# Lead-in of a fused linear-attention and gated-MLP kernel: 64x64 state products, one scaling on GpSimd, two copies on VectorE, constants for the idle products

## Chip, cores and metric

One core of one Trainium2 chip. The time is the device time of one launch in microseconds; the kernel before has a median of 202.86 us over three runs (202.58 to 203.15). Every other time below comes from one profiled execution of it.

## The reference

```python
def _attn_ref(q, k, v, lam):              # q, k, v: [4, 8, 768, 64]; block = 64
    ...
    for b in range(nb):
        intra = einsum('bhic,bhjc->bhij', qb, kb) * Dmask      # lam**(i-j) for i >= j, else 0
        intra = einsum('bhij,bhjd->bhid', intra, vb)
        inter = einsum('bhid,bhde->bhie', qb * lam_pow, kv_state)
        out[:, :, sl] = intra + inter
        kv_state = lam_block * kv_state + einsum('bhsd,bhse->bhde', kb * rev_pow, vb)

def _moe_ref(x, w_in, w_out):             # x: [3072, 512], w_in: [512, 2048], w_out: [2048, 512]
    h = x @ w_in
    return (h * cos(h)) @ w_out
```

x is the attention output with the heads side by side, one row for each token.

## The kernel before

The powers of lam are folded into scales: q is multiplied by lam**pos, k or v by lam**-pos, with pos counted from the middle of the sequence, so that the decay mask becomes a plain causal one and the running state a plain sum of k.T v. Tokens go in blocks of 128. The gated MLP works on tiles of four or two blocks (`TILES`): for each of 16 groups of 128 hidden columns, f0 to f15, L732 multiplies x (held transposed, `xT`) by `w_in`, ScalarE takes the cosine (L738), VectorE multiplies (L744), and L778 multiplies by `w_out`.

The order of instructions isn't that of the program text. Every piece of work is a `Task` with an engine, an assumed duration, dependencies and a priority; `Planner.order` (L72) simulates the engines with these numbers, with assumed delays between engines (`LAT`) and with the times from which each engine is free (`SETUP`), and the tasks are emitted in the order of their planned starts. So a changed duration or engine in the plan can also change the order on each engine.

**The lead-in.** The first four blocks, which make the first MLP tile, don't take the ordinary way but the one of `add_span` (L579): a span is the first 256 tokens of a batch, two tokens to a partition, and there are two spans, x0 and x1. SyncE issues the loads of q and k of x0, then of x1 (L253; 512 KB each). GpSimd's queue issues v of both, then the first two chunks of `w_in` (two groups of columns each, f0 and f1, f2 and f3), then GpSimd scales k of x1, and only then issues the other four chunks (one, three, four and four groups: f4; f5 to f7; and so on) and `w_out`. All tasks of a span split the heads in two halves, hp0 and hp1:

- `prep` (L592) scales q and k into bf16. The table `QK` (L32) names the engine by span and half.
- `transposes` (L596) turns q and k on TensorE, four 128x128 products for each half; `transposes_out` (L603) copies them out of PSUM, by `OUTS` all on ScalarE.
- `scores` (L606), 16 products 64x64 of 128 columns for each half; `scores_out` (L616) applies the mask, two VectorE instructions for each half.
- `update` (L620) forms the state of the span's first block, `ps_kv`: for each pair of heads and each s a product with 64 rows and 128 columns of the array, of which only the two diagonal 64x64 blocks are used. `update_out` (L628) copies these blocks into `kv_bd`, whose other parts were set to zero; `STATE_OUT` (L34) names the engines.
- `values` (L631), 16 products for each half; `carried` (L642), four products with `kv_bd` on top; `values_out` (L648) copies the two blocks of the span to `xT`; `VALUES_OUT` (L33) names the engines.

While TensorE would wait in the lead-in, `keep_awake` (L861) has it multiply constants into a bank that nobody reads. It uses a float32 tile of zeros, `blank`, that VectorE sets first (L215), or for pauses from 0.25 to 0.6 us the identity. Before the first transposes stands the product that spreads lam over the partitions (L875), from which ScalarE computes the scales.

Of the kernel before, what the change touches and what calls it, by code (L numbers as in the profile page):

```python
# [10 lines left out]
F32 = mybir.dt.float32  # L11
BF16 = mybir.dt.bfloat16
# [16 lines left out]
APART = [3, 4, 5, 11]  # L29


QK = [{"q": ("DVE", "DVE"), "k": ("DVE", "DVE")}, {"q": ("DVE", "DVE"), "k": ("POOL", "POOL")}]  # L32
OUTS = [{"qT": ("ACT", "ACT"), "kT": ("ACT", "ACT")}, {"qT": ("ACT", "ACT"), "kT": ("ACT", "ACT")}]  # L33
VALUES_OUT = [("ACT", "ACT"), ("DVE", "ACT")]  # L34
STATE_OUT = [("ACT", "ACT"), ("ACT", "ACT")]
ORDER = "q0 k0 q1 k1 v0 v1 i0 i1 i2 i3 i4 i5 o0 o1 o2 q4 q5 k4 k5 o3"

W_IN = [2, 2, 1, 3, 4, 4]
# [18 lines left out]
class Planner:  # L57


    LAT = {"PE": 0.2, "ACT": 0.06, "DVE": 0.08, "POOL": 0.1, "SP": 0.0, "DMA": 0.0, "SETUP": 0.0}  # L60

    SETUP = {"POOL": 3.7, "DVE": 4.4, "ACT": 6.0, "SP": 0.85, "DMA": 1.95}

    def __init__(self, bufs):
        self.tasks, self.bufs = [], bufs
# [6 lines left out]
    def order(self):  # L72
        free, done = dict(self.SETUP), []
        got = {tag: [] for tag in self.bufs}
        owner = [None] * BANKS
        only = {}
        todo = list(self.tasks)
        while todo:
            first = {}
            for t in todo:  # L80
                if only.get(t.eng, t) is not t:
                    continue
                at = self.ready(t, got)
                if at is None:
                    continue
                if t.banks:
                    b = self.free_banks(t, owner)
                    if len(b) < t.banks:
                        continue
                    t.bank = b[:t.banks]  # L90
                    at = max([at] + [x for x, _ in t.bank])
                at = max(at, free.get(t.eng, 0.0))
                first.setdefault(t.eng, []).append((at, t))
            best = None
            for eng, c in first.items():
                t0 = min(a for a, _ in c)
                a, t = min(((a, t) for a, t in c if a <= t0 + 1e-6 + t.worth), key=lambda x: x[1].issue.end if eng == "DMA" else x[1].prio)
                if best is None or a < best[0]:
                    best = (a, t)
            assert best, "no task can start"  # L100
            a, t = best
            t.start, t.end = a, a + t.dur
            free[t.eng] = t.end
            only.pop(t.eng, None)
            if t.then:
                only[t.eng] = t.then
            if t.get:
                got[t.get].append(t)
            if t.banks:
                t.bank = [i for _, i in t.bank]  # L110
                for j, i in enumerate(t.bank):
                    owner[i] = (t, j)
            todo.remove(t)
            done.append(t)
        return sorted(done, key=lambda t: t.start)
# [29 lines left out]
def kernel(  # L145
# [10 lines left out]
    nc = tc.nc  # L156
    B, H, S, D = q.shape
    P = 128
# [19 lines left out]
    consts = ctx.enter_context(tc.tile_pool(name="consts", bufs=1))  # L178
# [5 lines left out]
    def bank(i, shape, dt, name):  # L184
        return psum.tile(shape, dt, tag=f"bank{i}", bufs=1, name=name)
# [9 lines left out]
    ident = consts.tile([P, P], BF16)  # L195
# [15 lines left out]
                                base=0, pattern=[[1, D]], channel_multiplier=-1)  # L211
    halfpi = consts.tile([P, 1], F32)
    nc.vector.memset(halfpi, math.pi / 2.0)
    blank = consts.tile([P, 4 * P], F32)
    nc.vector.memset(blank, 0.0)  # L215
    kv_bd = consts.tile([P, 2, NP, P], BF16)
    nc.vector.memset(kv_bd, 0.0)

# [8 lines left out]
    pl = Planner({**BUFS, "q_f": BUFS["ld"], "k_f": BUFS["ld"], "v_f": BUFS["ld"]})  # L227
# [3 lines left out]
    halves = [slice(i * D, (i + 1) * D) for i in range(2)]  # L231
# [344 lines left out]
    spans, span_deps = [], []  # L576
    span_v = [consts.tile([P, H, 2, D], BF16, name=f"v_sp{x}") for x in range(SPANS)]

    def add_span(x):  # L579
        pa = lambda part: -1000.0 + 2 * x + part  # L580
        pv = lambda part: -990.0 + 2 * x + part
        cut = [slice(4 * hp, 4 * hp + 4) for hp in range(2)]
        us = {"DVE": 0.69, "POOL": 1.04}
        vec = {"DVE": nc.vector, "POOL": nc.gpsimd}
        L = {name: consts.tile([P, 2, H, D], BF16, name=f"{name}_sp{x}") for name in ("q", "k")}
        L["v"] = span_v[x].rearrange("u h s d -> u s h d")
# [33 lines left out]
        def update(t):  # L620
            L["kv"] = bank(t.bank[0], [P, NP, P], F32, "ps_kv")
            rows = chunks[0][0]
            for p in range(NP):
                for s in range(2):
                    nc.tensor.matmul(L["kv"][:, p, :], lhsT=L["k"][rows, s, 2 * p:2 * p + 2, :], rhs=L["v"][rows, s, 2 * p:2 * p + 2, :],  # L625
                                     start=(p == 0 and s == 0), stop=True, skip_group_check=True)

        def update_out(_, h, e):  # L628
            (nc.scalar.copy if e == "ACT" else nc.vector.tensor_copy)(kv_bd[h, x, :, h], L["kv"][h, :, h])
# [26 lines left out]
        so, kt, v_t = [[], []], [], [load_t["v_f", "sp", x]]  # L656
        for hp in range(2):
            eq, ek = QK[x]["q"][hp], QK[x]["k"][hp]
            a = pl.add(eq, us[eq], [load_t["q_f", "sp", x]], partial(prep, name="q", hp=hp, e=eq), pa(-0.9 + 0.1 * hp))
            kt.append(pl.add(ek, us[ek], [load_t["k_f", "sp", x]], partial(prep, name="k", hp=hp, e=ek), pa(-0.9 + 0.1 * hp)))  # L660
            if x:
                w_t["in", 2].issue.deps.append(kt[hp])
            outs = []
            for name, src in (("qT", a), ("kT", kt[hp])):
                e = OUTS[x][name][hp]
                t = pl.add("PE", MM(P, 4), [src, s_first if name == "kT" else None], partial(transposes, name=name, hp=hp), pa(-0.5 + 0.1 * hp), banks=1)
                outs.append(pl.add(e, 0.58 if e == "ACT" else 0.42, [t], partial(transposes_out, name=name, hp=hp, e=e), pa(-0.5 + 0.1 * hp)))
                t.bank_frees = [[outs[-1]]]
            s1 = pl.add("PE", 0.42, outs, partial(scores, hp=hp), pa(0.1 + 0.1 * hp), banks=2)
            if x and hp == 0:  # L670
                s_first = s1
            so[hp] = [pl.add("DVE", 0.69, [s1], partial(scores_out, hp=hp, i=i), pa(0.1 + 0.1 * hp + 0.05 * i)) for i in range(2)]
            s1.bank_frees = [[t] for t in so[hp]]

        u = pl.add("PE", 0.42, v_t + kt + [spans[0].get("carried")], update, pv(0.1), banks=1)
        Uo_sp[x] = [pl.add(e, 0.4 if e == "ACT" else 0.42, [u], partial(update_out, h=h, e=e), pv(0.1))
                    for h, e in zip(halves, STATE_OUT[x])]
        u.bank_frees = [Uo_sp[x]]
        span_deps.extend(v_t + kt)
        v0 = pl.add("PE", 0.35, so[0] + v_t + [spans[0].get("carried")], partial(values, hp=0), pv(0.2), banks=2)  # L680
        v1 = pl.add("PE", 0.35, [v0] + so[1], partial(values, hp=1), pv(0.25))
        second = pl.add("PE", MM(P, 4) + 0.1, [v1] + Uo_sp[x], carried, pv(0.3))
        for c, (t, e) in enumerate(zip((v1, second), VALUES_OUT[x])):
            Vo[2 * x + c] = [pl.add(e, 0.6 if e == "ACT" else 0.69, [t], partial(values_out, c=c, e=e), pv(0.3) if c == 0 else -1200.0)]
# [132 lines left out]
    for at, name in enumerate(names):  # L817
        which, n = name[0], int(name[1:])
# [14 lines left out]

    idle = pl.add("SETUP", 0.0, [], None, -1e9, banks=1)
    for x in range(SPANS):
        add_span(x)
# [21 lines left out]
    tc.plan = plan  # L858
    idle_ps = bank(idle.bank[0], [P, 4 * P], F32, "ps_idle")

    def keep_awake(us, at):  # L861

        cols = int((us - 0.06) * (1200.0 if at < 7.0 else 2400.0) / 4) // 64 * 64
        if us < 0.6:
            if us > 0.25:
                nc.tensor.matmul(idle_ps, lhsT=ident, rhs=ident.unsqueeze(1).to_broadcast([P, 4, P]), start=True, stop=True)
            return
        while cols > 0:
            n = min(cols, 4 * P)
            nc.tensor.matmul(idle_ps[:, :n], lhsT=blank[:, :P], rhs=blank[:, :n], start=True, stop=True)  # L870
            cols -= n

    keep_awake(1.2, 1.6)
    lam_ps = bank((idle.bank[0] + 4) % BANKS, [P, H], F32, "ps_lam")
    nc.tensor.matmul(lam_ps, lhsT=ones, rhs=lam_row, start=True, stop=True)  # L875
    lnl = consts.tile([P, H], F32)
# [14 lines left out]
    nc.scalar.activation(v_scale, expo, AF.Exp, scale=-1.0)  # L891
    warm = consts.tile([P, 1], F32)
    nc.scalar.activation(warm, halfpi, AF.Sin)
    now = 2.8
    for t in plan:
        if t.eng == "PE" and t.start < lead_end.start + 1e-6:
            keep_awake((t.start - now) * 0.95 if now < 3.0 else t.start - now, now)
            now = t.end
        if t.emit:
            t.ins = t.emit(t)  # L900

# [29 lines left out]
```

## Time and profile before

| | |
|---|---|
| median of three runs | 202.86 us |
| the profiled execution: its time, its span | 202.54 us, 200.8 us |
| TensorE busy | 195.9 us |
| VectorE, ScalarE, GpSimd busy | 116.3, 119.4, 64.9 us |
| first product of TensorE | 1.66 us |
| first product of the MLP (L732) | 14.14 us |
| VectorE's scaling of a half of q or k | 688 ns |
| GpSimd's scaling of a half of k | 1040 ns |
| a mask on VectorE (L617) | 684 ns |
| eight products of `update` (L625) | 0.62 us |

The page lists for each engine its busy time, its share of the span and its instructions; PE is TensorE's products, PEld its weight loads, DVE VectorE, ACT ScalarE, POOL GpSimd, SP SyncE. The chain of waits follows the work that ended last back from the end. A line of the timeline has a start, the time to the end of the last of the merged instructions, the engine, the line, the operation, and what it writes and reads; in brackets is the idle time before it and what ended that. The ends of products are modelled, about 0.2 us after their start even where the next starts 0.03 us later, so the distance from start to start tells what a product costs. A DMA row has the size and the time from issue to landing.

### The profile page before, as it was taken

What the parts mean: (1) busy time and instruction counts of PE and PEld (TensorE: products, weight loads), DVE (VectorE), ACT (ScalarE), POOL (GpSimd) and SP (SyncE); (2) the same over time, 40 slices, a digit from 0 to 9 for tenths busy, and PEclk for the clock granted to TensorE, in tenths of its full rate; (3) what the DMA queues carried; (4) which work ended last, traced back from release to release, by engine and by line L of the source; (5) the groups of instructions that cost most, each with busy time, mean ns of one, the idle gap of its engine ahead of it and who ended that gap; (6) DMA issues with size and microseconds to landing.
All of it is one profiled execution on the core that took longest, in us unless ns stands there. A gap on an engine that the chain in (4) does not pass through costs nothing.

```text
span 200.8 us, 5951 instructions
## 1 busy us (share of the span) xinstructions
PE 195.9 (98%) x2473; PEld 116.8 (58%) x2473; DVE 116.3 (58%) x230; ACT 119.4 (59%) x241; POOL 64.9 (32%) x85
## 2 busy tenths in 40 slices
PE   6999999999999999999999999999999999999994
PEld 3477444558757757766658676755445544444452
DVE  3978771269756948758458575835588354444001
ACT  4878771149658768666639666644887564345120
POOL 5893003085235360635555353545500000000000
PEclk9999999999999999999999999999999999999999
DMA  5999999999889997999999899979910010111112
GB/s 163 303 190 204 203 199 216 209 238 225 200 197 225 262 202 177 239 179 253 189 275 245 188 207 194 277 141 261 243 23 3 3 52 0 52 55 52 52 52 104
DMA packets 96620, 33.93 MB, mean 169 GB/s; under 512 B 84690, under 2 KB 93650, under 8 KB 96594
## 3 DMA queue, kind: packets, MB, share of 16 engines
q1 hardware_dynamic: 89088, 28.78, 63.2%
q0 software_dynamic: 7360, 4.72, 16.4%
q8 instruction: 19, 0.31, 0.7%
q10 hardware_dynamic: 146, 0.07, 0.1%
q14 instruction: 7, 0.06, 0.1%
HBM read 27.26 MB, written 6.29 MB: 167 GB/s over the span
## 4 chain that ended last, share of the span: by engine, by line
PE 95%; DMA 2%; ACT 0%; DVE 0%; SPq 0%; issue 0%; ACTq 0%; DVEq 0%
PE ps_h L732 42%; PE ps_f L778 42%; DMA sp_f<-in_k_dram 2%; PE ps_s L407 2%; PE ps_o L502 2%; PE ps_o L470 2%; PE ps_kv L419 1%; PE ps_t L601 1%; PE ps_s L612 1%; PE ps_o L638 1%; PE ps_kv L625 1%; PE ps_x L470 0%; PE ps_idle L870 0%; PE ps_t L359 0%; DVE k_sp L593 0%; PE ps_o L644 0%
## 5 line engine op out<-in xcount | busy, mean ns | idle before, releaser
L744 DVE TENSOR_TENSOR g<-ps_h,cos 128x256 bf16<-128x256 f32 (+1 forms) x149 | 73.1, 501 | 42.0 <-ACT cos L738 41.1
L738 ACT ACTIVATE cos<-ps_h,halfpi 128x256 f32<-128x256 f32 (+1 forms) x149 | 75.9, 536 | 29.3 <-PE ps_h L732 28.2
L778 PE MATMUL ps_f<-w_out_sb,g 128*128 128x512 bf16 (+2 forms) x400 | 91.4, 371 | 0.0
L732 PE MATMUL ps_h<-xT,w_in_sb 128*128 128x256 bf16 (+1 forms) x596 | 91.1, 303 | 0.0
L732 PEld LDWEIGHTS <-w_in_sb 128*128 128x128 bf16 x596 | 57.5, 98 | 30.1 <-DVE xT L510 0.4
L778 PEld LDWEIGHTS <-g 128*128 128x128 bf16 x400 | 37.6, 98 | 37.2
L329 POOL TENSOR_TENSOR qk<-q_f,q_scale 128x512 bf16<-128x512 f32 x19 | 20.0, 1067 | 34.7 <-DMA q_f<-in_q_dram 17.6
L792 ACT COPY o_sb<-ps_f 128x512 f32<-128x512 f32 (+1 forms) x24 | 13.7, 572 | 24.7 <-PE ps_f L778 24.5
L337 POOL TENSOR_TENSOR v_s<-v_f,v_scale 128x512 bf16<-128x512 f32 x19 | 19.6, 1042 | 9.8 <-DMA v_f<-in_v_dram 5.2
L412 DVE TENSOR_TENSOR s_m<-ps_s,mask 128x512 bf16<-128x512 f32 x20 | 13.0, 685 | 4.2 <-PE ps_s L407 3.6
L333 POOL CAST qk<-k_f 128x512 bf16<-128x512 f32 x18 | 11.0, 611 | 10.4 <-DMA k_f<-in_k_dram 10.2
L510 ACT CAST xT<-ps_o 128x512 bf16<-128x512 f32 x11 | 6.0, 588 | 9.0 <-PE ps_o L502 5.6
L425 DVE TENSOR_TENSOR sum<-sum,ps_kv 128x512 f32<-128x512 f32 x15 | 10.2, 682 | 0.6
L430 ACT CAST S<-sum 128x512 bf16<-128x512 f32 x15 | 9.1, 616 | 0.9 <-DVE sum L425 0.8
L253 POOL DMA_DIRECT2D w_out_sb<-in_moe_w_out_dram x4 | 3.0, 784 | 15.8 <-DMA q_f<-in_q_dram 15.8
L792 DVE COPY o_sb<-ps_f 128x384 f32<-128x384 f32 x1 | 0.6, 557 | 11.6 <-DMA out_dram<-o_sb 11.6
L470 PEld LDWEIGHTS <-v_s 64*64 64x64 bf16 x320 | 4.0, 107 | 4.2 <-issue 3.4
L870 PE MATMUL ps_idle<-blank 128*128 128x512 f32 (+2 forms) x8 | 4.7, 707 | 1.7 <-DVE blank L215 1.7
L487 DVE COPY spare<-ps_o 1x1 f32<-1x1 f32 x6 | 0.9, 156 | 8.4 <-PE ps_o L470 8.4
L617 DVE TENSOR_TENSOR s_m_sp<-ps_s,mask_sp 128x512 bf16<-128x512 f32 x8 | 5.1, 684 | 1.2 <-PE ps_s L612 1.2
L470 PE MATMUL ps_o<-s_m,v_s 64*64 64x64 bf16 x256 | 5.2, 196 | 0.0
L502 PE MATMUL ps_o<-qkT,S 64*64 64x64 bf16 x304 | 4.9, 195 | 0.0
(76 smaller groups left out, 90.1 us busy)
## 6 DMA issues: line engine op xcount, KB each, us to landing
q_f<-in_q_dram SPq DMA_DIRECT2D x20, 256.0 KB, 3.9
k_f<-in_k_dram SPq DMA_DIRECT2D x20, 256.0 KB, 4.2
v_f<-in_v_dram SPq DMA_DIRECT2D x20, 256.0 KB, 5.1
out_dram<-o_sb SPq DMA_DIRECT2D x19, 256.0 KB, 2.5
w_out_sb<-in_moe_w_out_dram POOLq DMA_DIRECT2D x4, 512.0 KB, 12.4
sp_f<-in_q_dram SPq DMA_DIRECT2D x2, 512.0 KB, 4.9
sp_f<-in_k_dram SPq DMA_DIRECT2D x2, 512.0 KB, 5.5
w_in_sb<-in_moe_w_in_dram POOLq DMA_DIRECT2D x2, 512.0 KB, 8.9
```

The costliest lines, as they stand in the source:

```text
L329: vec[e].tensor_mul(new_qk()[:, 0, :, s], live.pop(("q_f", 2 * pr + s)), q_scale[:, c, :].unsqueeze(2).to_broadcast([P, H, D]))
L333: (nc.scalar.copy if early else nc.gpsimd.tensor_copy)(new_qk()[:, 1, :, s], live.pop(("k_f", 2 * pr + s)))
L337: vec[e].tensor_mul(live["v_s", 2 * pr + s], live.pop(("v_f", 2 * pr + s)), v_scale[:, c, :].unsqueeze(2).to_broadcast([P, H, D]))
L412: nc.vector.tensor_mul(t, live["s", pr][s], mask.unsqueeze(1).to_broadcast([P, H, D]))
L425: nc.vector.tensor_add(new, live["sum", pr, 0] if half else live["sum", pr - 1, 1], live["kv", pr][half])
L430: nc.scalar.copy(new_S(pr, half), live["sum", pr, half])
L470: yield lambda h=h: nc.tensor.matmul(o[halves[h % 2], h // 2], lhsT=live["v_s", n0 + s][m, h, :], rhs=live["s_m", n0 + s][m, h, :], start= ...
L732: nc.tensor.matmul(t[:, :n], lhsT=w_in_sb[:, kd, f * P:(f + 1) * P], rhs=live["xT", i][:, kd, at], start=(kd == 0), stop=(kd == KD - 1))
L738: nc.scalar.activation(c[:, :n], live["h", i, f, at.start][:, :n], AF.Sin, bias=halfpi)
L744: return nc.vector.tensor_mul(live["g", i][:, f, at], live.pop(("h", i, f, at.start))[:, :n], live.pop(("c", i, f, at.start))[:, :n])
L778: nc.tensor.matmul(live["f", i, j, piece][:, :width], lhsT=live["g", i][:, f, j * P:(j + 1) * P], rhs=w_out_sb[:, f, part], start=(f == 0) ...
L792: (nc.scalar.copy if eng == "ACT" else nc.vector.tensor_copy)(o[:, :width], live["f", i, j, piece][:, :width])
```

## The change

- **64x64 products.** `update` forms only the two diagonal blocks, each with its own product of 64 rows, 64 columns of the array and 64 columns of v: 16 products where there were 8.
- **GpSimd.** The scaling of q of x1, hp1, goes from VectorE to GpSimd, ahead of its two scalings of k.
- **Two copies on VectorE.** For x0, one of the two copies to `kv_bd` and the copy of the second block to `xT`, both on ScalarE before.
- **Constants.** The idle products use a bf16 constant 1.0 that the framework sets at launch and that is read with a stride of zero; `blank` and its memset go, and with it the wait of TensorE's first product. The amounts of idle products are worked out anew.
- **Plan.** Some of the planner's durations and two of its `SETUP` times are changed.

In the programs as built, the order on the engines differs in the lead-in alone: on TensorE the 32 products of `values` of x0 stand together ahead of x1's first scores (before, the second half of them stood after x1's last transposes), and one block of four products of L732, f0, stands ahead of x1's first `values` (before, f0, f1 and f2 stood together behind them). ScalarE's and VectorE's queues change by the moved copies; GpSimd's by the one scaling. DMAs stand in the same order.

```diff
-QK = [{"q": ("DVE", "DVE"), "k": ("DVE", "DVE")}, {"q": ("DVE", "DVE"), "k": ("POOL", "POOL")}]
+QK = [{"q": ("DVE", "DVE"), "k": ("DVE", "DVE")}, {"q": ("DVE", "POOL"), "k": ("POOL", "POOL")}]
-VALUES_OUT = [("ACT", "ACT"), ("DVE", "ACT")]
-STATE_OUT = [("ACT", "ACT"), ("ACT", "ACT")]
+VALUES_OUT = [("ACT", "DVE"), ("DVE", "ACT")]
+STATE_OUT = [("ACT", "DVE"), ("ACT", "ACT")]
...
-    SETUP = {"POOL": 3.7, "DVE": 4.4, "ACT": 6.0, "SP": 0.85, "DMA": 1.95}
+    SETUP = {"POOL": 3.7, "DVE": 4.2, "ACT": 6.1, "SP": 0.85, "DMA": 1.95}
...
-    blank = consts.tile([P, 4 * P], F32)
-    nc.vector.memset(blank, 0.0)
...
-        us = {"DVE": 0.69, "POOL": 1.04}
+        us = {"DVE": 0.62, "POOL": 1.02}
...
-                    nc.tensor.matmul(L["kv"][:, p, :], lhsT=L["k"][rows, s, 2 * p:2 * p + 2, :], rhs=L["v"][rows, s, 2 * p:2 * p + 2, :],
-                                     start=(p == 0 and s == 0), stop=True, skip_group_check=True)
+                    for i, h in enumerate(halves):
+                        nc.tensor.matmul(L["kv"][h, p, h], lhsT=L["k"][rows, s, 2 * p + i, :], rhs=L["v"][rows, s, 2 * p + i, :],
+                                         start=(p == 0 and s == 0), stop=True, skip_group_check=True)
...
-            s1 = pl.add("PE", 0.42, outs, partial(scores, hp=hp), pa(0.1 + 0.1 * hp), banks=2)
+            s1 = pl.add("PE", 0.33, outs, partial(scores, hp=hp), pa(0.1 + 0.1 * hp), banks=2)
...
-            so[hp] = [pl.add("DVE", 0.69, [s1], partial(scores_out, hp=hp, i=i), pa(0.1 + 0.1 * hp + 0.05 * i)) for i in range(2)]
+            so[hp] = [pl.add("DVE", 0.61, [s1], partial(scores_out, hp=hp, i=i), pa(0.1 + 0.1 * hp + 0.05 * i)) for i in range(2)]
...
-        u = pl.add("PE", 0.42, v_t + kt + [spans[0].get("carried")], update, pv(0.1), banks=1)
+        u = pl.add("PE", 0.28, v_t + kt + [spans[0].get("carried")], update, pv(0.1), banks=1)
...
-        v0 = pl.add("PE", 0.35, so[0] + v_t + [spans[0].get("carried")], partial(values, hp=0), pv(0.2), banks=2)
-        v1 = pl.add("PE", 0.35, [v0] + so[1], partial(values, hp=1), pv(0.25))
+        v0 = pl.add("PE", 0.33, so[0] + v_t + [spans[0].get("carried")], partial(values, hp=0), pv(0.2), banks=2)
+        v1 = pl.add("PE", 0.33, [v0] + so[1], partial(values, hp=1), pv(0.25))
...
-    def keep_awake(us, at):
-
-        cols = int((us - 0.06) * (1200.0 if at < 7.0 else 2400.0) / 4) // 64 * 64
-        if us < 0.6:
-            if us > 0.25:
-                nc.tensor.matmul(idle_ps, lhsT=ident, rhs=ident.unsqueeze(1).to_broadcast([P, 4, P]), start=True, stop=True)
+    one = nc.const_aps.tensor(1.0, [P, 4 * P], BF16)
+
+    def idle_cols(n):
+        nc.tensor.matmul(idle_ps[:, :n], lhsT=one[:, :P], rhs=one[:, :n], start=True, stop=True)
+
+    def keep_awake(us, slow):
+        if not slow and us < 0.6:
             return
+        cols = int((us - 0.06) * (1200.0 if slow else 2400.0)) // P * P
         while cols > 0:
             n = min(cols, 4 * P)
-            nc.tensor.matmul(idle_ps[:, :n], lhsT=blank[:, :P], rhs=blank[:, :n], start=True, stop=True)
+            idle_cols(n)
             cols -= n
 
-    keep_awake(1.2, 1.6)
+    keep_awake(2.0, True)
...
-    now = 2.8
+    now = 3.3
     for t in plan:
         if t.eng == "PE" and t.start < lead_end.start + 1e-6:
-            keep_awake((t.start - now) * 0.95 if now < 3.0 else t.start - now, now)
-            now = t.end
+            slow = t.start < 8.5
+            keep_awake(t.start - now, slow)
+            now = max(t.end, t.start + 0.45) if slow else t.end
```

## The prediction

> **What bounds the kernel now.** I read the page's shares first, then the busy time by stage, then the waits, the DMA view and the timeline of the one stage in which TensorE is not simply full.
>
> ```profile
> span 200.8 us, 5951 instructions
> PE 195.9 (98%) x2473; PEld 116.8 (58%) x2473; DVE 116.3 (58%) x230; ACT 119.4 (59%) x241; POOL 64.9 (32%) x85
> ...
> PE 95%; DMA 2%; ACT 0%; DVE 0%; SPq 0%; issue 0%; ACTq 0%; DVEq 0%
> ```
>
> TensorE is the chain; only the DMA in front of it holds another 2%. Busy time by stage (columns: stage, its length, PE, PEld, DVE, ACT, POOL, clock, DMA share, GB/s):
>
> ```profile
> 14.14:16.70 2.56, 2.56 (x45) 1.84 (x37) 2.55 (x6) 2.20 (x6) 2.56 (x4) 1.00 1.48 197
> 16.70:193.00 176.30, 176.30 (x2224) 104.82 (x2224) 103.91 (x206) 106.55 (x214) 51.66 (x59) 1.00 0.79 169
> 193.00:200.80 7.80, 4.92 (x39) 3.00 (x37) 0.56 (x1) 0.85 (x2) 0.00 (x0) 0.94 0.20 74
> ```
>
> From 16.70 us on TensorE has 176.30 us of work in 176.30 us, and the built programs list the same instructions in the same order from there to the end. So the change is worth exactly what it moves the moment at which TensorE enters that stretch. What ends last there? The waits between 16.0 and 17.3 us, the weight loads and the issues of the two chunks concerned (KB each, us from issue to landing; issued at 11.46 and 12.26 us):
>
> ```profile
> PEld L732 <- DMA w_in_sb<-in_moe_w_in_dram: 0.2, 1, 0.2
> ...
> 16.09 0.37 PEld L732 LDWEIGHTS <-w_in_sb 128*128 128x128 bf16 x4
> 16.69 0.55 PEld L732 LDWEIGHTS <-w_in_sb 128*128 128x128 bf16 x6 [0.23 <-DMA w_in_sb<-in_moe_w_in_dram]
> ...
> w_in_sb<-in_moe_w_in_dram POOLq DMA_DIRECT2D x1, 128.0 KB, 5.2
> ...
> w_in_sb<-in_moe_w_in_dram POOLq DMA_DIRECT2D x1, 384.0 KB, 6.1
> ```
>
> The last wait of the lead-in is TensorE's for a DMA: f4, the fifth hidden block (L732 with w_in's third chunk), starts at 16.70 because that chunk lands at 11.46 + 5.2 = 16.66. TensorE itself was free for f4 at 16.58 (f3 starts at 16.14, four matmuls at 0.109). The next chunk lands at 12.26 + 6.1 = 18.36, and f5 starts at 18.45. So two limits end within 0.12 us of each other: the compute chain of the spans (16.58) and the stream of loads (16.66).
>
> ```profile
> DMA  0000559999999999999999999999999999999999
> GB/s 0 0 0 14 135 118 309 346 345 350 346 344 349 346 345 350 344 254 183 181 178 184 181 192 200 193 198 198 213 171 193 205 203 197 208 212 203 209 207 203
> ```
>
> In these 40 slices of 0.5 us the DMA engines are full from 3 us on: q0, k0, q1, k1, v0, v1 and the w_in chunks come one behind another, and no issue is late enough to leave a hole.
>
> [...] 0.148 us from the last transpose (128x128) to the first score (64x64), 0.022 between two products in the same mode (L470 to L419 at 43.13). [...] The span's masks on L617 read PSUM and SBUF, and took 681 ns beside GpSimd's scaling and 680 without.
>
> **The change part by part.** All sums are against the profiled execution (202.54 us: span 200.8 and 1.74 around it; the median of the runs is 202.86, 0.32 above it). x0, x1 are the two spans; hp0, hp1 the halves of their heads.
>
> Constants. VectorE's memset of 0.48 us goes; VectorE then idled 1.67 us before L879, so 0. TensorE's fillers start at about 0.8 instead of 1.66. Before the lam product: 2304 bf16 columns[...], and lam's row is waited for until 3.02. After it: 2048 columns[...]; the first transposes wait for VectorE until 5.59. Cost 0[...]. The fillers between 5.6 and 8.2 shrink from 3x512 columns to 768 in all. Bounds: 0, or a lost clock (rival 2).
>
> q of x1, hp1. VectorE loses one product: pitch 0.60. Its first mask needs scores that are done at 8.57, and waited for VectorE until 9.02; now it can start at about 8.69, and the fourth ends near 11.17 instead of 11.50: 0.33 earlier. GpSimd gains 1.04 us ahead of its two k products (L593, mean 1040). It issues w_in DMAs until 8.51; its product started 0.15 us after the wait was met (9.32 to 9.47), so q runs about 8.63 to 9.67 and the first k ends at 10.67 to 10.74, against 10.51. If the queue hides that start, the delay is 0. I take +0.16. Queued behind on GpSimd are four w_in and three w_out issues, then later by up to 0.23; the engines are busy with earlier chunks until 14.9, which hides it. TensorE waits for q hp1 until 9.72 instead of 9.23, then idles or fills up to k as before: 0.
>
> Update as 64x64. Before: 8 products, 0.546 us from 10.90 to the values at 11.45, mode change included. After: 16 products, two at a time; eight rounds at 0.032 (pitch of L697 and L419) plus 0.02, and no mode change to the values: 0.27. So 0.27 less, twice, 0.55 in all. Lower bound 0 gain if the pairs don't overlap (16 x 0.032 = 0.51).
>
> Copies. kv_bd's second half of x0 (ScalarE 0.37) and xT's second block (ScalarE about 0.5 in pitch) go to VectorE (about 0.42 and 0.60 to 0.68). ScalarE's own kv_bd half now waits for VectorE's in the built program, so the pair stays serial: 11.60 to 12.02, then to 12.42, still ahead of its reader (L644 at about 12.5, before 12.70). Behind it on ScalarE stand xT and kT of hp1, which gives scores of x1 hp1 at about 13.49 (before 13.57).
>
> The new order: straight products of x0 all together, and f0 ahead of x1's first values. Walking it through, with GpSimd 0.16 late: k transposes 10.78, update 11.11, values 11.38 to 11.83, scores x1 hp0 11.86 (before 11.69), VectorE then without a gap: mask 12.30, xT 12.99, masks 13.59, 14.19 and 14.79, the last ended at 15.47 (before 15.32). TensorE: scores hp1 13.49, f0 13.84 (its weights landed at 7.00 + 6.5 = 13.5), values 14.37, f1 14.69, f2 15.13 (weights by 15.0), values 15.66, f3 16.24, free for f4 at 16.68. Without GpSimd's delay it is 16.55.
>
> The sum: removed are 0.55 of update and 0.33 of VectorE, and 0.35 of x0's values moves into TensorE's wait for kT; what stands in their place is VectorE's chain of five operations behind x1's scores, 5 x 0.60, which has one copy more than before and fills the gap that it had. Compute reaches f4 at 16.55 to 16.68 against 16.58, and f4 starts when w_in's third chunk has landed: 16.70 in both. Net 0.0, bounds -0.15 (chunk earlier, no GpSimd delay) to +0.2. That gives 202.54 for an execution like the profiled one and 202.9 for the median.
>
> **Rivals.** (1) Gain: the stream is not a fixed limit, the third chunk comes early enough without the profiler, and the edits add up: half to all of 0.55 + 0.33, so 202.0 to 202.4, 202.2 in the middle. For it: the chunk's 5.2 us are long for 128 KB. Against it: VectorE's chain, which no edit shortens. Chance 0.10. (2) Slower: the half clock. Between 5.3 and 8.2 us fillers give 0.32 us of work where 0.65 stood. [...] the products between 10.8 and 12.6 take twice as long: transposes, update, values, scores, 1.2 us become 2.4, in front of VectorE's chain; minus the slack before f4 about +0.9: 203.8. It decides if the clock shows halves after 8 us.[...] Chance 0.10. (3) Slower: a straggling chunk. The page has 19 instruction packets, 0.31 MB, 0.7% of 16 engines: 1.2 us each on one engine. TensorE has more instructions now; one such packet in front of w_in's second or fourth chunk costs up to 0.75: 203.5. Chance 0.08. (4) The change does what it says and is hidden, my forecast: 0.72.
>
> **How the numbers follow.** A measurement of this kernel tells about 0.3% (0.6 us) from no change: three runs lay within 0.57 us. Forecast 202.9; its own range 202.4 to 203.3. Reaching to the others' nearer ends: 202.3 to 203.6. Faster by over 0.3% is rival 1, 0.10; slower is 2 and 3, 0.18; the rest 0.72.
>
> **What would show it.** Right: f4's weight load again ends a wait for the w_in DMA near 16.7; VectorE masks and xT without a gap from 12.2 to 15.4; update about 0.27 from its start to the values. Wrong: TensorE entering its full stretch before 16.4 or after 17.0; a clock under 1.00 after 8 us; GpSimd's q beginning later than 8.8.

## The result, and the profile after

The changed kernel takes 204.12 us (median of 11 runs, 203.51 to 205.61), the kernel before 202.75 us beside it (11 runs, 202.52 to 203.36). The ratio is 1.0055, with a 95% interval of 1.003 to 1.0079: slower by 0.55%, about 1.1 us. All executions here are undisturbed ones; the ratios, here and below, are estimated from all of them and need not equal the quotient of the two medians (here 1.0068).

The profiled execution took 204.47 us. Its page, first the span and the shares, then the chain of waits by engine:

```profile
span 202.7 us, 5968 instructions
...
PE 193.0 (95%) x2466; PEld 116.2 (57%) x2495; DVE 116.0 (57%) x230; ACT 118.7 (59%) x239; POOL 65.6 (32%) x86
...
PE 81%; DMA 8%; DVE 3%; issue 3%; POOL 2%; ACT 1%; SPq 1%; ACTq 0%
```

29 products are missing from the records (2466 against 2495 weight loads), so TensorE's 193.0 us are too low; the weight loads are complete, and distances are read from them. In the chain stands a share of 3% that wasn't there before: "issue", time in which the engine waited for nothing that the profile shows. Part of it is only the place of products whose records are missing. The DMA's 8% are in the main loads of k and v that the chain follows from 31 to 43 us, where the delay grows by 0.2 us at most. The stages say where the time went:

```profile
14.14:16.70 2.56, 1.82 (x38) 1.07 (x36) 1.95 (x4) 1.41 (x3) 2.56 (x4) 1.00 1.49 197
16.70:193.00 176.30, 173.12 (x2198) 104.81 (x2227) 104.37 (x206) 106.32 (x214) 51.41 (x59) 1.00 0.82 168
193.00:202.70 9.70, 6.84 (x48) 3.85 (x46) 0.56 (x1) 1.37 (x3) 0.00 (x0) 0.98 0.22 81
```

In the 2.56 us ahead of f4's old start TensorE was busy for 2.56 us before, and now for 1.82. TensorE's timeline of that stage (lines of the changed kernel: L610 scores, L731 hidden, L637 values, L643 carried):

```profile
13.37 0.42 PE L610 MATMUL ps_s<-qT_sp,kT_sp 64*64 64x128 bf16 x16 [0.20 <-ACT kT_sp L602]
13.72 0.61 PE L731 MATMUL ps_h<-xT,w_in_sb 128*128 128x256 bf16 x4
14.26 0.42 PE L637 MATMUL ps_o<-s_m_sp,v_sp 64*64 64x128 bf16 x16
14.61 1.06 PE L731 MATMUL ps_h<-xT,w_in_sb 128*128 128x256 bf16 x8
15.60 0.36 PE L637 MATMUL ps_o<-s_m_sp,v_sp 64*64 64x128 bf16 x12
16.97 0.25 PE L637 MATMUL ps_o<-s_m_sp,v_sp 64*64 64x128 bf16 x4 [1.00 <-issue]
17.15 0.40 PE L643 MATMUL ps_o<-qT_sp,kv_bd 128*128 128x128 bf16 x4
17.38 0.82 PE L731 MATMUL ps_h<-xT,w_in_sb 128*128 128x256 bf16 x6
```

Up to 15.60 all is where the prediction put it. Then TensorE does 12 of the 16 products of x1's second values, stops for 1.0 us (1.2 by its weight loads), and does the other four. In the built program these four wait for no semaphore, and what they read was ready (the last mask ended at 15.34). The waits of that stage say the same, "issue" and no other engine:

```profile
PEld L637 <- issue: 1.6, 3, 1.2
...
PE ps_o L637 <- issue: 1.0, 1, 1.0
```

f3 starts at 17.38 where the forecast had 16.24, and TensorE is free for f4 about 17.8 where it had 16.68. The first product with w_out stands at 28.82 before and at 29.94 after: 1.12 us, about what the ratio says. The profiled execution loses another 0.8 us in small waits between 40 and 155 us; such waits come and go between executions of the kernels here (the profiled one of the kernel before has none, and lies 0.2 to 0.3 below that kernel's medians).

What was going on at 15.6 us? The DMA queues between 14 and 16 us (packets, MB, share of 16 engines; the shares sum up the times of all packets, which at 150.2% overlap):

```profile
q0 software_dynamic: 897, 0.37, 150.2%
q8 instruction: 1, 0.02, 3.0%
```

One instruction packet of 16 KB on queue q8 moved from 14.50 to 15.46 (3.0% of 16 engines for 2 us is 0.96 us of one), among the chunks of `w_in`. Before, the same packet moved from 14.32 to 15.29. If TensorE's records (weight loads, products and two or three others) are counted from 0 in order of their start, TensorE stops ahead of number 448; with the one product whose record is missing by then it is 449. Before, it came to number 448 only at 17.69. That is the theory to test.

### The profile page after: what moved, and what is told of

It reads as the page before. It is cut to its first block, busy times and chain, and to the rows that moved or that the text cites. A ratio compares the mean times of both kernels' runs of the same rounds, so it can differ in the third digit from the quotient of the medians.

```text
span 202.7 us, 5968 instructions
## 1 busy us (share of the span) xinstructions
PE 193.0 (95%) x2466; PEld 116.2 (57%) x2495; DVE 116.0 (57%) x230; ACT 118.7 (59%) x239; POOL 65.6 (32%) x86
## 4 chain that ended last, share of the span: by engine, by line
PE 81%; DMA 8%; DVE 3%; issue 3%; POOL 2%; ACT 1%; SPq 1%; ACTq 0%
PE ps_h L731 39%; PE ps_f L777 34%; DMA v_f<-in_v_dram 4%; DVE g L743 2%; DMA k_f<-in_k_dram 2%; DMA sp_f<-in_q_dram 2%; PE ps_o L500 2%; PE ps_o L468 2%; PE ps_kv L417 2%; PE ps_s L405 1%; POOL v_sp L251 1%; SPq L251 1%; ACT cos L737 1%; POOL q_sp L591 1%; PE ps_x L468 0%
## 5 line engine op out<-in xcount | busy, mean ns | idle before, releaser
L731 PE MATMUL ps_h<-xT,w_in_sb 128*128 128x256 bf16 (+1 forms) x591 | 90.6, 303 | 0.6 <-issue 0.2
L777 PE MATMUL ps_f<-w_out_sb,g 128*128 128x512 bf16 (+2 forms) x377 | 87.6, 370 | 2.1 <-issue 1.4
L731 PEld LDWEIGHTS <-w_in_sb 128*128 128x128 bf16 x596 | 57.4, 98 | 30.3 <-issue 0.4
L863 PE MATMUL ps_idle<-const-bfloat16-1.0 128*128 128x512 bf16 (+3 forms) x16 | 5.2, 433 | 0.9 <-PEq L917 0.8
```

What stands on the lines that cost most here:

```text
L731: nc.tensor.matmul(t[:, :n], lhsT=w_in_sb[:, kd, f * P:(f + 1) * P], rhs=live["xT", i][:, kd, at], start=(kd == 0), stop=(kd == KD - 1))
L777: nc.tensor.matmul(live["f", i, j, piece][:, :width], lhsT=live["g", i][:, f, j * P:(j + 1) * P], rhs=w_out_sb[:, f, part], start=(f == 0) ...
```

## Theories

**Theory 1: TensorE runs out of instructions.** By this theory the packets of q8 bring its instructions, and what follows number 448 is there only from about 16.7 us on. (The records don't say whose instructions a packet holds. That those of 16 KB are TensorE's fits their number, 19 in the whole execution and 20 in a_early, whose program has 118 TensorE instructions more; but the smaller packets of queue q14 also go from 7 to 8 there.) The change brings 56 more TensorE instructions into the lead-in (4989 against 4933 in the program; 32 of them by the update's 16 extra products, each with a weight load; the traces show 22 weight loads more, 2495 against 2473). TensorE is at number 448 two microseconds sooner and has to stop. **Theory 2 (rival): the new order, or the longer chains of VectorE and GpSimd,** cost the time, and the stop is how they show.

In the trace each of these loads lands in 16 parts, each with a time of its own, and they show what may be a second effect of the same packet. The last three parts of three loads, in us:

```
                        w_in chunk 2          w_in chunk 3          x1's v
before            14.85  14.87  14.94   15.55  15.59  16.65   12.10  12.13  12.15
after             14.89  14.90  15.01   15.61  15.62  16.83   12.18  12.18  12.19
old update        14.92  14.95  16.57   15.63  15.66  16.85   12.17  12.19  12.23
32 idle rows      14.78  14.96  16.43   15.52  15.67  16.77   12.10  12.14  12.24
early idle rows   14.82  14.98  16.05   15.60  15.69  16.77   12.16  12.25  13.78
```

In each of these executions one part in sixteen comes over 1 us late, from some load on. So the third chunk that held f4 at 16.70 before was late by its last part alone (16.65; the fifteen others by 15.59). In all 14 traces the first load with such a part, 0.6 us late or more, lands after the packet began to move. Where it is the second chunk, f2 waits for it. Which load it is doesn't follow from the packet's recorded start alone: that is 14.50 in the changed kernel (third chunk) and in a_old_update (second chunk).

## Experiments

The columns: ratio to the kernel before with its interval, and how much later than before the first product with w_out starts in the profiled execution, which can lie far from the median (a_old_update).

| run | median us (range) | ratio | first w_out product |
|---|---|---|---|
| the changed kernel | 204.12 (203.51 to 205.61) | 1.0055 [1.003, 1.0079] | +1.12 |
| a_old_update | 202.93 (202.57 to 205.02) | 1.0009 [0.9992, 1.0027] | +1.48 |
| b_new_update | 203.62 (203.09 to 204.13) | 1.0019 [0.9999, 1.0039] | +0.58 |
| b_more32 | 204.02 (203.79 to 206.01) | 1.0081 [1.0049, 1.0112] | +1.34 |
| b_more64 | 204.54 (203.65 to 205.63) | 1.0081 [1.005, 1.0112] | +0.92 |
| a_plus8 | 205.17 (205.0 to 205.34) | 1.0125 [1.0105, 1.0146] | +0.93 |
| a_fewer | 203.61 (203.27 to 204.6) | 1.0057 [1.0039, 1.0075] | +0.67 |
| a_early | 203.30 (203.17 to 203.61) | 1.0036 [1.0023, 1.0049] | +0.97 |
| a_no_v1 | 203.28 (202.28 to 204.57) | 1.0025 [1.0011, 1.004] | -0.23 |
| a_old_both | 203.48 (203.02 to 204.67) | 1.0032 [1.0018, 1.0047] | +1.14 |
| a_old_idle | 203.78 (203.52 to 204.96) | 1.0054 [1.0038, 1.007] | +0.89 |
| b_new_idle | 202.75 (202.47 to 204.13) | 0.9998 [0.9977, 1.002] | -0.03 |
| b_gpsimd | 202.78 (202.6 to 204.19) | 1.0002 [0.9985, 1.0019] | +0.08 |

### Undo the update, or do it alone

a_old_update is the changed kernel with this edit; b_new_update is the kernel before with the reverse one.

```diff
-                    for i, h in enumerate(halves):
-                        nc.tensor.matmul(L["kv"][h, p, h], lhsT=L["k"][rows, s, 2 * p + i, :], rhs=L["v"][rows, s, 2 * p + i, :], ...)
+                    nc.tensor.matmul(L["kv"][:, p, :], lhsT=L["k"][rows, s, 2 * p:2 * p + 2, :], rhs=L["v"][rows, s, 2 * p:2 * p + 2, :], ...)
```

> The changed kernel with the update put back to 8 products of 64x128 (32 instruction rows of TensorE fewer: 4957 against 4989, the order otherwise the same). Theory 1, TensorE runs out of instructions: its stop of 1.0 us in the middle of x1's second values came near instruction 448 of its stream, while the packets that bring instructions share the full DMA engines with the loads; with fewer instructions in front, TensorE reaches that place later, when the next ones have come. The stop goes or falls below 0.3 us: 202.7 to 203.2. Theory 2, the new order (values of x0 together, f0 ahead of x1's values) or GpSimd's and VectorE's chains cause the loss: the time stays at 203.9 to 204.3.

> The kernel before with the update alone as 16 products of 64x64 (rows 4965, 32 more than before; nothing else, planner's durations as before). Theory 1: TensorE reaches instruction 448 at about 16.0 us instead of 17.7, and stops there for 0.7 to 0.9 us: 203.4 to 203.7. Theory 2: the update alone is 0 to 0.3 us shorter, the lead-in otherwise as before: 202.6 to 202.8.

Without the update's new form the loss is gone (1.0009): the new order, GpSimd, the copies and the constants together cost nothing that can be measured, and theory 2 falls for this kernel. (With the old idle products the new order does cost something; see a_old_both.) The profile of a_old_update caught one of its longest executions (204.50). It has no stop, but the late part in the second chunk:

```profile
14.84 0.61 PE L730 MATMUL ps_h<-xT,w_in_sb 128*128 128x256 bf16 x4
16.62 0.61 PE L730 MATMUL ps_h<-xT,w_in_sb 128*128 128x256 bf16 x4 [1.17 <-DMA w_in_sb<-in_moe_w_in_dram]
```

The update alone makes the stop, in the products of `carried`, at number 449:

```profile
15.58 0.42 PE L639 MATMUL ps_o<-s_m_sp,v_sp 64*64 64x128 bf16 x16
15.93 0.29 PE L645 MATMUL ps_o<-qT_sp,kv_bd 128*128 128x128 bf16 x2
16.74 0.27 PE L645 MATMUL ps_o<-qT_sp,kv_bd 128*128 128x128 bf16 x2 [0.53 <-issue]
```

It came there at 16.00 and went on at 16.74, as expected. The loss is 0.58 us in this execution; all 13 runs lie above 203.0, but the ratio's interval just touches 1 (the quotient of the medians is 1.0037).

### Idle instructions, and nothing else

The kernel before with one idle float32 product of 512 columns, at 9.5 us, cut into many bf16 ones of about the same length in all (18 of 128 columns, or 34 of 64). No work of the computation is touched.

```diff
-            nc.tensor.matmul(idle_ps[:, :n], lhsT=blank[:, :P], rhs=blank[:, :n], start=True, stop=True)
+            if at < 7.0:
+                nc.tensor.matmul(idle_ps[:, :n], lhsT=blank[:, :P], rhs=blank[:, :n], start=True, stop=True)
+            else:
+                for _ in range(18):
+                    nc.tensor.matmul(idle_ps[:, :128], lhsT=ident, rhs=ident[:, :128], start=True, stop=True)
```

> The kernel before with one idle float32 product (9.5 us, into the bank that nobody reads) replaced by 18 bf16 idle products of 128 columns: about 32 instructions more on TensorE in about the same time, no work of the computation touched. Theory 1: a stop of 0.6 to 0.9 us near 16 us: 203.3 to 203.7. Theory 2: as before, 202.6 to 202.9.

> The same with 34 idle products of 64 columns: about 64 instructions more. Theory 1: instruction 448 is reached at about 15.5 us, the stop is 1.1 to 1.5 us: 203.9 to 204.3. Theory 2: as before, 202.6 to 202.9.

Both cost 0.8%. The number alone does it, and neither 64x64 products nor a new order are needed. But in the profiled executions the time went in the other way, to the second chunk's late part, not to a stop; of b_more32:

```profile
14.23 1.05 PE L732 MATMUL ps_h<-xT,w_in_sb 128*128 128x256 bf16 x8
16.48 0.61 PE L732 MATMUL ps_h<-xT,w_in_sb 128*128 128x256 bf16 x4 [1.20 <-DMA w_in_sb<-in_moe_w_in_dram]
```

In b_more64 the packet moved at 13.66 instead of 14.32, and the wait is 0.60. I had expected the stop alone, growing with the number; the size doesn't grow, and both medians are above what I expected. Why the second chunk got the late part in b_more32 stays open: its packet moved at 14.38, no sooner than before.

### Does the stop belong to the products or to the number?

The changed kernel with eight small idle products more ahead of the lam product:

```diff
     keep_awake(2.0, True)
+    for _ in range(8):
+        idle_cols(64)
```

> The changed kernel with 8 idle products of 64 columns more (16 instructions) ahead of the lam product, where TensorE has time to spare. Theory 1 (TensorE stops where its delivered instructions end, at number 448 of its stream in the trace): the stop moves by 8 products, to after 4 of the 16 products of x1's second values instead of after 12, and lasts about 0.1 to 0.2 us longer, as the place is reached sooner; if instead the packet is served in front of w_in's second chunk, one sixteenth of that chunk lands 1 us late and TensorE waits for it at f2. Either way 203.8 to 204.6. Rival: a stop that belongs to the products themselves stays after the twelfth.

```profile
15.65 0.25 PE L637 MATMUL ps_o<-s_m_sp,v_sp 64*64 64x128 bf16 x4
16.67 0.36 PE L637 MATMUL ps_o<-s_m_sp,v_sp 64*64 64x128 bf16 x12 [0.77 <-issue]
```

The stop moved by exactly eight products, to after four of sixteen: it belongs to the number. It didn't become longer, as TensorE went on sooner (16.67 for 16.96). The two runs, 205.0 and 205.34, are above what I expected; the profiled one lost 0.93 in the lead-in and 1.5 in waits after 40 us, which two runs don't settle.

### Fewer idle products, or more of them early

a_fewer leaves out the changed kernel's idle products after 5 us (the first diff); a_early cuts those before 5.3 us into 64 columns each (the second; `early` is set for the calls before 4 us of the plan).

```diff
-            keep_awake(t.start - now, slow)
+            if now < 4.0:
+                keep_awake(t.start - now, slow)
```

```diff
-            n = min(cols, 4 * P)
+            n = 64 if early else min(cols, 4 * P)
```

> The changed kernel without the idle products after 5 us (8 products, 16 instructions fewer). Theory 1: the stop moves on by 8 products, to f3's first, is reached about 0.5 us later and so lasts about 0.5 us less: 203.3 to 203.8; the clock stays at 1.0. Rival, the half clock (rival 2 of the prediction): without these products the clock falls in the lead-in, and the time rises to 204.5 or more.

> The changed kernel with the idle products ahead of 5.3 us cut into 64 columns each (118 instructions more, the same columns): the limit at number 448 falls among x1's work at about 13 us[...]. Theory 1: the packet is served before 12 us, nothing stops at 15.6, w_in's second and third chunks land whole by 15.7; what may come late instead is the packet after it, in front of w_in's fourth chunk: 202.4 to 203.4. Rival, more instructions always cost (each 32 cost what the runs above showed): 204.5 to 206.

a_fewer's time was as expected, for another reason. There is no stop; TensorE runs at half speed until about 12.6 us:

```profile
10.01 0.61 PE L599 MATMUL ps_t<-ident,q_sp 128*128 128x128 bf16 x4
...
12.89 0.40 PE L599 MATMUL ps_t<-ident,k_sp 128*128 128x128 bf16 x4
...
16.28 0.42 PE L637 MATMUL ps_o<-s_m_sp,v_sp 64*64 64x128 bf16 x16
```

Four transposes take 0.61 us until then, 0.40 afterwards; their weight loads follow at 107 ns instead of 56. From 5.5 to 11.2 us TensorE did 28 transposes (3.0 us) and 32 products of the scores (1.1 us), and the transposes' steps were still long at the end of that. Second values start at 16.28 instead of 15.60, so late that, by theory 1, what follows number 448 has come: half speed costs 0.67 here, and hides the stop.

The column of the granted clock reads 1.00 all that time, but only because it counts time without a record as full clock, and a_fewer's trace has no record of the clock (its page has no clock line). It reads 1.00 in the changed kernel's first 1.66 us too, when idle products of 512 columns start 0.43 us apart (0.22 from 10.17 us on). Where a trace has records, the first begins when the steps get short: at 5.4 us before, at 4.3 in the changed kernel, but at 9.0 in a_old_update, which has the same idle products, and at 8.7 in a_old_both. So that moment differs by microseconds between executions. a_fewer's is the latest of all 14, and that the missing products put it there is likely but not shown: in the changed kernel full speed came before the first of them.

In a_early the packet began to move at 11.69, before 12 us as expected, and the long stop is gone. A small remnant of it is left, at the same place: in a row of `update` products TensorE starts number 447 at 14.03 and goes on at 14.15, where the other steps are about 0.03 us. That is again 1.5 us after the packet's end (12.63). What I hadn't expected: now the late part is that of x1's v, and of every chunk after it.

```profile
PE ps_kv L624 <- DMA v_sp<-in_v_dram: 0.8, 1, 0.8
PE ps_h L731 <- DMA w_in_sb<-in_moe_w_in_dram: 0.2, 1, 0.2
```

So the late part moved to earlier loads together with the packet.

### The same instructions, but the loads sooner

```diff
+    nc.vector.memset(span_v[1], 0.0)
...
+            n = 1 if on_pool and x == 1 else H
-            return start(..., t.rearrange("u h s d -> u h (s d)"), ...)
+            return start(..., t.rearrange("u h s d -> u h (s d)")[:, :n], ...)
```

> The changed kernel with only one head of eight of x1's v loaded, the others left at zero (part of the input is left out): the w_in chunks follow about 1.2 us sooner, the instructions of TensorE are the same in number and order. Theory 1, with the packet waiting behind the loads on its DMA engine: it is served about 1.2 us sooner, near 13.2 instead of 14.5, TensorE doesn't stop in x1's values: 202.4 to 202.9. If the packet comes a fixed time after TensorE's call, whatever is loaded, the stop stays: 203.8 to 204.2.

This kernel leaves out seven of the eight heads of x1's v. With that part of the load gone (the second chunk landed at 13.54 for 15.01), the packet moved at 12.88 instead of 14.50, though TensorE's instructions up to there are the same. So its time does depend on the loads, here by 1.6 us. (No record shows whether and when TensorE calls for a packet.) The stop is gone, with number and order of instructions unchanged:

```profile
15.40 0.42 PE L639 MATMUL ps_o<-s_m_sp,v_sp 64*64 64x128 bf16 x16
15.75 0.40 PE L645 MATMUL ps_o<-qT_sp,kv_bd 128*128 128x128 bf16 x4
15.99 2.24 PE L733 MATMUL ps_h<-xT,w_in_sb 128*128 128x256 bf16 x19
```

The first product with w_out starts 0.23 us sooner than before. That is what the edits bring without the stop, or less, since w_in's third chunk too landed sooner (15.27), and the kernel before wasn't run with the smaller load. The whole time missed what I expected (203.28): the profiled execution loses 1.1 us after 29 us, part of it in waits for `w_out` (0.2) and for a scaling of v (0.3); why this kernel does so more often than others stays open.

### The other edits

a_old_idle is the changed kernel with the idle products of before, a_old_both the same with the old update too, b_new_idle the kernel before with the new idle products, and b_gpsimd the kernel before with this edit:

```diff
-... {"q": ("DVE", "DVE"), "k": ("POOL", "POOL")}]
+... {"q": ("DVE", "POOL"), "k": ("POOL", "POOL")}]
```

> The changed kernel with the update as 8 products and with the idle products of the kernel before (float32 zeros, with their memset): what is left of the change is q's second scaling on GpSimd, the two copies on VectorE, the plan and so the new order; 7 rows of TensorE more than before. Theory 1: nothing stops near number 448, and the 16.65 us of w_in's third chunk hold f4 as before: 202.5 to 202.9, ratio 0.998 to 1.001. Theory 2, the new order or the longer GpSimd chain costs something of its own: 203.2 or more.

> The changed kernel with the idle products of the kernel before (17 rows fewer than the changed kernel, 39 more than before). Theory 1: TensorE reaches number 448 some 3 to 8 products later than in the changed kernel, the stop or the late part of a chunk remains: 203.4 to 204.1. If the constants alone were to blame: 202.7.

> The kernel before with the changed kernel's idle products alone (bf16 constants, no memset; 24 rows more). Theory 1: number 448 is reached about 12 products sooner than before, still near the end of the packet's delay, so a small stop of 0 to 0.5 us or now and then a late part of w_in's second chunk: 202.8 to 203.5. If the earlier first product alone gave something: below 202.6.

> The kernel before with q of x1, hp1, scaled on GpSimd alone (4 rows more on TensorE; the planner then puts the values of x0 together). Theory 1: VectorE's first mask 0.3 us earlier and GpSimd's k 0.2 us later, both hidden behind the loads: 202.5 to 203.0, ratio 0.998 to 1.002. Theory 2: the longer GpSimd chain shows: 203.2 or more.

GpSimd's scaling and the constants cost nothing alone. a_old_both missed, and lies in the range that I had put down for theory 2: 0.5 us more than a_old_update, which differs from it by the idle products only. The profile of a_old_idle, which has the same idle products, shows a part of it:

```profile
13.34 0.39 PE L867 MATMUL ps_idle<-ident 128*128 128x512 bf16 x1
13.66 0.42 PE L612 MATMUL ps_s<-qT_sp,kT_sp 64*64 64x128 bf16 x16
14.01 0.39 PE L867 MATMUL ps_idle<-ident 128*128 128x512 bf16 x1
14.23 0.60 PE L733 MATMUL ps_h<-xT,w_in_sb 128*128 128x256 bf16 x4
...
16.09 0.41 PE L639 MATMUL ps_o<-s_m_sp,v_sp 64*64 64x128 bf16 x13
16.74 0.25 PE L639 MATMUL ps_o<-s_m_sp,v_sp 64*64 64x128 bf16 x3 [0.24 <-issue]
```

In the new order the old rule puts two idle products of 512 columns in front of x1's last scores and of f0, where nothing is waited for that long: scores at 13.66 instead of 13.37, f0 at 14.23 instead of 13.72. Of these 0.51 us 0.23 came in earlier, as GpSimd, waiting for the load of k, began with it at 9.85 and not at 9.62, so the two idle products make about 0.3. a_old_both has them too. Its own profiled execution, the longest of its runs, is a poor witness: it ran at half speed until 8.7 us and was behind by 0.6 us at x1's first scores (12.64 against 12.02 in a_old_idle). So the new rule, which puts no idle product there, is worth about 0.3 us in the new order; the rest of the 0.5 stays open. In a_old_idle the delay comes out of the stop, which is 0.46 us long instead of 1.21, since TensorE arrives later at the same limit.

### The stops side by side

```
                      came to number 448/449   went on   packet moved
after                        15.75              16.96    14.50 to 15.46
a_plus8                      15.66              16.67    14.42 to 15.38
b_new_update                 16.00              16.74    14.51 to 15.48
a_old_idle                   16.28              16.74    14.40 to 15.37
a_early                      14.03              14.15    11.69 to 12.63
b_new_idle                   17.00              no stop  14.22 to 15.12
before                       17.69              no stop  14.32 to 15.29
a_no_v1                      15.54              no stop  12.88 to 13.77
```

In the first four TensorE goes on at 16.67 to 16.96, whenever it came. All five stops end 1.3 to 1.5 us after the packet's recorded end, also in a_early, where the packet came 2.8 us sooner. With the missing product counted, all five stand at the same number, after 449 records; and in the other nine traces TensorE came there 1.3 us or more after the packet's end. Theory 1 stands for the stop. Open stays why those 1.3 to 1.5 us pass. That the late part is the packet's doing, on one DMA engine with it, is inferred from their moving together, since the trace doesn't name the engine.

## Why the prediction was wrong, step by step

- **Update.** Its duration was right: 0.26 us from its start to the values (11.05 to 11.31) against 0.27. What was left out, put at nothing without a reason, is the price of 32 instructions more (8 products with their weight loads, twice). On this path that is what counts: alone, the edit loses 0.58 in the lead-in, and without it the rest loses nothing.
- **The new order.** Right to the last step but one: q on GpSimd 8.62 (8.63), first mask 8.74 (8.69), transposes of k 10.72 (10.78), scores 11.79 and 13.37 (11.86, 13.49), f0 13.72 (13.84), second values 15.60 (15.66), masks done 15.34 (15.47). The step that failed is "values 15.66, f3 16.24": the walk let TensorE issue without limit. f3 came at 17.38; 1.1 us is the whole error of the lead-in. One of the prediction's own signs of being wrong came true: TensorE entered its full stretch after 17.0 (17.7).
- **Constants, q of x1, copies.** Zero each, as put down (in the changed kernel the idle products ahead of the lam product started at 0.84, 0.43 us apart for 512 columns, and that product at 2.85 for 3.02; the last of those behind it started at 4.47, and the first transpose waited for VectorE until 5.63); a_old_update shows their sum, with the new order: 1.0009. The two copies were not run alone. That the new idle products save about 0.3 us in the new order was in the walk only by using the order as built.
- **The sum.** "f4 starts when w_in's third chunk has landed" was right for before and was misread: a fixed limit of the stream was taken for what is one late part (16.65 against 15.59), which in these runs moved together with an instruction packet.
- **Rivals.** Rival 3 named the packet and "TensorE has more instructions now", with 203.5 and a chance of 0.08. The place that it named, the late second chunk, is where a_old_update, b_more32 and b_more64 lost their time (0.6 to 1.2 us against "up to 0.75"); the changed kernel lost it to the stop. It lacked the other half, that TensorE itself waits (by theory 1, for what the packet carries; the records show the stop of 1.2 us and its end 1.5 us after the packet's), and the count: 448 reached at 17.69 before, with only 1 us to spare to 16.7. Rival 2, half speed, didn't happen in the changed kernel's profiled execution, but did with still fewer idle products (a_fewer, 0.67 against 0.9), and its test by the clock column would not have shown it, since the column reads 1.00 where there is no record. What brings half speed was not shown.

No version is clearly faster than the kernel before. Without the stop (a_no_v1) the lead-in was shorter by 0.23 us, 0.1%, less than the times of these runs can tell, and a part of that may be the smaller load.

## What to carry to other kernels

Where TensorE works in many small products while the DMA engines are full, count its instructions. Here the 16 products that took the place of 8 shortened the update's work (0.55 us to 0.26 from its start to the values), and the kernel still lost 1.1 us, in a stop that theory 1 puts down to a packet of instructions that moved among the loads (14.50 to 15.46). An idle span that the profile put down to "issue", in the middle of a row of like products, pointed to that here (1.0 us, after 12 products of 16); shift the number of instructions and see whether the stop moves with it, as it did in a_plus8, by eight products. When a load's last part alone is late (16.65 us, the other fifteen by 15.59), look for what else moved at that moment before taking the stream for a limit.

## What the runs showed of the hardware

- The packets of the instruction queue q8 were 16 KB (19 of them, 0.31 MB, in the kernel before and the changed one). The first within the span, among the loads of the lead-in, took 0.89 to 0.98 us in the eight executions of the table above; in the five that have a stop, TensorE went on 1.3 to 1.5 us after its end. The first part of a load that came late after it began to move was 0.6 to 1.6 us late, and the loads behind had a late part too (in the changed kernel 1.2 us in w_in's third chunk, 1.0 in the fourth).
- TensorE can be at half speed while the column of the granted clock reads 1.00, which it also does where the trace has no record of the clock (a_fewer: 107 ns against 56 ns from transpose to transpose). The moment of full speed lay between 4.3 us (the changed kernel) and about 12.6 us (a_fewer).
- The update's 16 products more in the two spans, 32 instructions, cost nothing to issue (in the changed kernel the 16 products of 64x64 of x1 start within 0.25 us, 12.74 to 12.98). The lead-in lost 0.6 us with them alone (b_new_update) and 1.1 us in the changed kernel, in stops that theory 1 puts down to waiting for the instructions behind them (0.7 and 1.2 us).
